# Linear attention and a SoLU block: chunks 5 to 8 computed on token rows, with a new order table

## The chip, the cores and the metric

The kernel runs on one core of a Trainium2 chip. Times are device microseconds of one execution. The engines named below are TensorE (PE; PEld is its weight load), VectorE (DVE), ScalarE (ACT), GpSimd (POOL) and SyncE (SP). POOL and SP also issue DMAs, and each runs its instructions in the order in which they stand.

## The reference

```python
def _attn_ref(q, k, v, g_norm):                    # (8, 8, 576, 64) each
    kv = np.einsum('bhsd,bhse->bhde', k, v)
    out = np.einsum('bhsd,bhde->bhse', q, kv)
    rms = np.sqrt(np.mean(out * out, axis=-1, keepdims=True) + 1e-06)
    return (out / rms * g_norm).astype(np.float32)

def _moe_ref(x, w_in, w_out, g_ln):                # x (4608, 512), d_ff 1024
    h = x @ w_in
    e = np.exp(h - np.max(h, axis=-1, keepdims=True))
    solu = h * e / (np.sum(e, axis=-1, keepdims=True) + 1e-09)
    mu = np.mean(solu, axis=-1, keepdims=True)
    var = np.mean((solu - mu) ** 2, axis=-1, keepdims=True)
    return ((solu - mu) / np.sqrt(var + 1e-06) * g_ln) @ w_out
```
The attention's output, transposed to tokens by heads, is x. All inputs and the output are FP32.

## The kernel before

The 4,608 tokens are nine chunks of 512. Chunk c below 8 holds, of batch c, eight of every nine tokens; chunk 8 holds the ninth of every batch. Loads (one k, v and q for each batch, batches 0 and 1 in halves a and b) are issued by POOL and cast to BF16 on the way; only the first k and v come by SP and ACT.

Every step is a named piece of a plan: its engine, a function, what it needs and which buffer slot it takes. A long string, ORDER, lists the pieces, and each engine's instructions stand in that order; a slot behind "@" and an engine behind "/" choose the buffer and the engine. So the table, written out, is the schedule. PSUM has three slots P of two banks and two slots S of one; SBUF has slots L, M, osq, lss, rst and ob.

The names, for chunk c (lines of the kernel before):
- kv (L310) is k^T v of a batch, kc its copy to `kvd`. qt and qc turn q by TensorE in chunks 0 to 4; qx (L366) turns it by a DMA on SP in chunks 5 to 8. ql copies a batch's last tokens to `q_last` for chunk 8.
- o (L403) is q kv with features on partitions, in two halves; sq (L416) squares it on ACT, s (L431) takes the head's mean by a matmul with `head_mean`, ln (L435) and ex (L439) make the reciprocal root on ACT, x (L449) multiplies on DVE and gives BF16, features on partitions, as the next matmul wants it.
- h is x w_in: by features in chunks 0 to 2 (L489), by rows in chunks 3 to 8 (L498), in four pairs of halves of four matmuls each. e is exp (L508, L515), u = h exp(h) (L523, L528), r its squares (L538 to L548), g the sums of e on POOL (L559, chunks 0 to 2), z the column sums (L607), st and rs the statistics.
- t (L553) turns u of chunks 3 to 8 by a DMA on SP. `gate` (L339), a one-element copy on POOL, needs q7, the last load; t3.0, and behind it every DMA transpose, waits for it, so that transposes start when the loads have landed.
- a (L678) is u times the centred w_out: four row blocks of two pieces of four matmuls; b scales it, d stores it (L703; SP, POOL or ACT).
- warm (L204) runs matmuls of zeros while the first loads are under way; wm (L661) takes the mean of w_out's columns, wc (L664) subtracts it on DVE.

In a transposed u of chunk c, column block m holds rows 2m and 2m+1 of nine in turn, so a store of 128 rows writes two neighbouring rows for each of 64 groups.

Of the kernel before, what the change touches and what calls it, by code (L numbers as in the profile page):

```python
# [24 lines left out]
QUADRANTS = ()  # L25

# [36 lines left out]
WARM = (13, 6, 2, 1)  # L63
# [27 lines left out]
ex4.01@rst1 x4.01 h3.01 h3.10@P2 h3.11 e3.0@M10 u3.0@L5 e3.1@M8 u3.1 a2.11 b2.1/act@ob6 kv5@P1 kc5.1/dve r3.0/dve
r3.1/dve o4.1@P0 sq4.10@osq1 d0.3/pool sq4.11@osq0 a2.20@S1 kc5.0/act a2.21 kc5.2/act s4.10@S0 ln4.10@lss0 s4.11@P2
ln4.11@lss1 ex4.10@rst1 ex4.11@rst0 h3.20@P1 h3.21 x4.10 x4.11 e3.2@M8 u3.2 h3.30@P2 h3.31 h4.00@P0 h4.01 h4.10@P1
e3.3@M11 u3.3 r3.2/act t3.0 qx5@M10 ql0/dve e4.0@M9 u4.0@L3 h4.11 e4.1@M0 a2.30@S0 d1.0/pool b2.2/act@ob3 o5.0@P2
sq5.00@osq0 a2.31 sq5.01@osq1 o5.1@P0 sq5.10@osq2 s5.00@S1 u4.1 b2.3/dve@ob2 h4.20@P1 qx6@M1 t3.1 t3.2 ln5.00@lss1
t3.3 t4.0@L4 r3.3/dve st3 sq5.11@osq0 d1.1/sp d1.2/sp d1.3/sp s5.01@S0 d2.0/pool ln5.01@lss0 ex5.00@rst0 x5.00@M11
ex5.01@rst1 s5.10@S1 ln5.10@lss1 x5.01 t4.1 h4.21 a3.00@S0 a3.01 e4.2@M10 u4.2 t4.2 ex5.10@rst1 s5.11@S1 ln5.11@lss0
qx7@M5 x5.10 h4.30@P2 ex5.11@rst0 h4.31 e4.3@M2 a3.10@S1 d2.1/sp x5.11 d2.2/pool kv6@P1 kc6.2/dve a3.11 r4.0/act
h5.00@P0 kc6.0/act kc6.1/dve o6.0@P1 u4.3 rs3 b3.0/dve@ob4 b3.1/act@ob3 sq6.00@osq0 sq6.01@osq2 r4.1/dve h5.01
e5.0@M9 h5.10@P2 s6.00@S0 s6.01@S1 ln6.00@lss0 ln6.01@lss1 ex6.00@rst0 ex6.01@rst1 u5.0@L2 x6.00@M0 x6.01 h5.11  # L100
# [15 lines left out]
d5.3/pool d6.0/sp d6.1/pool h8.10@P2 h8.11 a7.10@S1 e8.0@M7 e8.1@M5 u8.0@L3 r8.0/act b7.0/act@ob0 a7.11 h8.20@P1
d6.2/pool h8.21 e8.2@M7 u8.1 u8.2 h8.30@P0 h8.31 e8.3@M0 t7.3 t8.0@L2 t8.1 t8.2 u8.3 a7.20@S0 d6.3/pool d7.0/pool
r8.1/dve r8.2/dve a7.21 t8.3 r8.3/act st8 rs8 b7.1/act@ob0 a7.30@P2 a7.31 b7.2/dve@ob4 a8.00@P0 a8.01 a8.10@P1
b7.3/act@ob5 b8.0/dve@ob3 a8.11 b8.1/dve@ob2 a8.20@S0 a8.21 a8.3|0@S1 a8.3|1@P1 b8.2/act@ob1 d7.1/pool d7.2/sp
d7.3/pool d8.0/sp b8.3|0/act@ob4 b8.3|1/dve@ob3 d8.1/act d8.2/sp d8.3|0/sp d8.3|1/sp  # L120
# [4 lines left out]
def kernel(  # L125
# [16 lines left out]
    nc = tc.nc  # L142
# [43 lines left out]
    zeros = big.tile([128, 512], BF16, name="zeros")
# [43 lines left out]
    plan.add("gr", "sp", load_g)  # L230
    plan.add("ident", "pool", make_ident)
# [438 lines left out]
    for f in range(NF):  # L670
        plan.add(f"wc{f}", "dve", lambda f=f: w_center(f), ["wm"], uses=["mean", ("w_out", f // 4)])
# [88 lines left out]
```

## Time and profile before

| | us |
|---|---|
| median of 3 runs | 183.61 (183.49 to 184.53) |
| the profiled execution | 184.59 |
| its span, first to last instruction | 182.8 |
| mean granted TensorE clock | 0.971 |
| HBM read, written | 32.51 MB, 9.44 MB |

The profile gives the busy time of each engine, the chain of work that ended last, and the waits. What lies between 184.59 and 182.8 is outside of the span. Times in it are us from the span's start; "L498" is a line of the kernel. The busy time of matmuls is larger than the time that they take in a row, because they are pipelined: the chain counts them by their distance.

### The profile page before, as it was taken

The page shows a single profiled execution, that of the slowest core. Times are in us where ns is not written, and L with a number is a line of the kernel's source. Part 1 is how long each engine was busy: PE and PEld are TensorE (multiplying, and loading weights), DVE is VectorE, ACT ScalarE, POOL GpSimd, SP SyncE. Part 2 cuts the span into 40 slices and gives each one's busy share as a digit, 9 for nine tenths or more (in the row PEclk, how much of TensorE's full clock was granted, in tenths as well). Part 3 has the DMA queues.
Part 4 walks back from the last instruction along what each step waited for, and adds up shares of the span by engine and source line. Part 5 has one row for each costly group of instructions (what it writes and reads, how often), then busy time and mean ns, then how long its engine had stood idle before and what let it go on. Part 6 is the DMA issues. An engine that isn't in the chain of part 4 may idle for free.

```text
span 182.8 us, 4297 instructions
## 1 busy us (share of the span) xinstructions
PE 167.0 (91%) x1719; PEld 82.0 (45%) x1739; DVE 123.0 (67%) x230; ACT 136.0 (74%) x249; POOL 61.1 (33%) x77
## 2 busy tenths in 40 slices
PE   7697977899999999999949999999999999999991
PEld 2342446445455556445413444544444444444450
DVE  1327586866594778678855769757986989765841
ACT  2349765979897878979856999997994787957350
POOL 7851696723695997001310010300000111211020
PEclk9979996999999999999996999999999999999999
DMA  5999999999999999996899999893254999837655
GB/s 172 248 206 280 338 208 209 205 208 212 253 207 232 208 207 208 207 208 105 233 177 221 240 227 227 237 185 71 77 105 71 251 237 209 225 117 157 130 199 203
DMA packets 53591, 36.19 MB, mean 198 GB/s; under 512 B 35580, under 2 KB 48644, under 8 KB 53572
## 3 DMA queue, kind: packets, MB, share of 16 engines
q0 software_dynamic: 15696, 21.17, 58.1%
q1 hardware_dynamic: 37460, 13.90, 36.8%
q10 hardware_dynamic: 416, 0.85, 1.4%
q8 instruction: 13, 0.21, 0.4%
q14 instruction: 6, 0.05, 0.1%
HBM read 32.51 MB, written 9.44 MB: 229 GB/s over the span
## 4 chain that ended last, share of the span: by engine, by line
PE 80%; DMA 8%; DVE 4%; ACT 3%; issue 3%; ACTq 0%; POOLq 0%
PE ps_S L678 27%; PE ps_P L498 21%; PE ps_P L489 11%; PE ps_P L678 6%; DMA sb_M<-sb_M 4%; DMA sb_M<-in_q_dram 4%; PE ps_P L403 3%; PE ps_S L431 3%; PE ps_P L310 3%; DVE sb_M L449 2%; PE ps_S L355 2%; PE ps_P L204 2%; PE ps_S L607 1%; DVE w_out_sb L664 1%; PE ps_P L431 1%
## 5 line engine op out<-in xcount | busy, mean ns | idle before, releaser
L678 PE MATMUL ps_S<-w_out_sb,sb_L 128*128 128x512 bf16 x220 | 54.4, 379 | 1.1 <-issue 0.8
L498 PE MATMUL ps_P<-w_in_sb,sb_M 128*128 128x512 bf16 x190 | 45.2, 385 | 0.2
L678 PEld LDWEIGHTS <-sb_L 128*128 128x128 bf16 x280 | 26.4, 98 | 31.4 <-issue 1.2
L528 DVE SCALAR_TENSOR_TENSOR sb_L<-ps_P,sb_M 128x1024 bf16<-128x1024 f32 x24 | 29.3, 1223 | 11.4 <-ACT sb_M L515 10.9
L703 POOL DMA_DIRECT2D out_dram<-sb_ob x17 | 10.5, 617 | 78.9 <-ACT sb_ob L693 31.2
L449 DVE SCALAR_TENSOR_TENSOR sb_M<-ps_P,g_cols,sb_rst 128x512 bf16<-128x512 f32 x36 | 27.0, 788 | 8.6 <-ACT sb_rst L439 7.4
L515 ACT ACTIVATE sb_M<-ps_P 128x1024 f32<-128x1024 f32 x24 | 24.5, 1022 | 6.9 <-PE ps_P L498 6.7
L498 PEld LDWEIGHTS <-sb_M 128*128 128x128 bf16 x192 | 18.9, 99 | 23.2 <-issue 1.8
L416 ACT ACTIVATE sb_osq<-ps_P 128x512 bf16<-128x512 f32 x36 | 20.0, 595 | 4.7 <-PE ps_P L403 4.6
L489 PE MATMUL ps_P<-sb_M,w_in_sb 128*128 128x512 bf16 x93 | 22.0, 379 | 0.4 <-issue 0.2
L523 DVE TENSOR_TENSOR sb_L<-ps_P,sb_M 128x1024 bf16<-128x1024 f32 x12 | 14.7, 1224 | 8.8 <-ACT sb_M L508 8.6
L439 ACT ACTIVATE sb_rst<-sb_lss 128x512 f32<-128x512 f32 x32 | 19.3, 631 | 0.4
L559 POOL TENSOR_TENSOR sb_M<-sb_M 128x512 bf16<-128x512 f32 x12 | 15.3, 1276 | 4.1 <-issue 2.2
L508 ACT ACTIVATE sb_M<-ps_P 128x1024 f32<-128x1024 f32 x12 | 12.3, 1023 | 4.5 <-PE ps_P L489 4.5
L548 DVE SCALAR_TENSOR_TENSOR sb_M<-sb_L 128x1024 bf16<-128x1024 bf16 x13 | 15.5, 1218 | 0.0
L695 DVE TENSOR_SCALAR sb_ob<-ps_S,rstd 128x512 f32<-128x512 f32 x15 | 11.2, 748 | 6.3 <-PE ps_S L678 5.4
L435 ACT ACTIVATE sb_lss<-ps_S 128x512 f32<-128x512 f32 x23 | 13.4, 594 | 2.0 <-PE ps_S L431 1.9
L489 PEld LDWEIGHTS <-w_in_sb 128*128 128x128 bf16 x96 | 9.0, 97 | 11.5 <-issue 1.8
L693 ACT ACTIVATE sb_ob<-ps_S,rstd 128x512 f32<-128x512 f32 (+1 forms) x15 | 10.1, 671 | 3.7 <-issue 1.8
L546 ACT ACTIVATE sb_M<-sb_L 128x1024 bf16<-128x1024 bf16 x11 | 11.6, 1053 | 1.3 <-DVE sb_L L528 1.3
L431 PE MATMUL ps_S<-sb_osq,head_mean 128*128 128x512 bf16 x26 | 9.9, 407 | 1.3 <-ACT sb_osq L416 1.2
L678 PE MATMUL ps_P<-w_out_sb,sb_L 128*128 128x512 bf16 x47 | 11.0, 379 | 0.1
(85 smaller groups left out, 178.8 us busy)
## 6 DMA issues: line engine op xcount, KB each, us to landing
out_dram<-sb_ob SPq DMA_DIRECT2D x17, 256.0 KB, 3.9
out_dram<-sb_ob POOLq DMA_DIRECT2D x17, 256.0 KB, 4.1
sb_L<-in_k_dram POOLq DMA_DIRECT2D x6, 576.0 KB, 16.4
sb_L<-in_v_dram POOLq DMA_DIRECT2D x6, 576.0 KB, 18.5
sb_M<-in_q_dram POOLq DMA_DIRECT2D x6, 576.0 KB, 17.3
sb_L<-in_moe_w_out_dram POOLq DMA_DIRECT2D x2, 1024.0 KB, 15.5
sb_M<-in_q_dram POOLq DMA_DIRECT2D x4, 288.0 KB, 11.1
w_in_sb<-in_moe_w_in_dram POOLq DMA_DIRECT2D x2, 512.0 KB, 11.1
```

Source lines behind the costliest of these rows:

```text
L416: nc.scalar.activation(out=t[:, :], in_=T["o", c, hf][:, z], func=AF.Square)
L431: nc.tensor.matmul(t[:, 0], head_mean[:, :], T["osq", i][:, :], start=True, stop=True)
L439: nc.scalar.activation(out=t[:, :], in_=T["lss", i][:, :], func=AF.Exp, scale=-0.5)
L449: nc.vector.scalar_tensor_tensor(out=T["x", c][:, pairs_of(c, hf), :, z], in0=T["o", c, hf][:, z].rearrange("p (n q) -> p n q", n=2), scal ...
L489: nc.tensor.matmul(t[:, f % 2], w_in_sb[:, dt, f * 128:(f + 1) * 128], T["x", c][:, dt].rearrange("p q z -> p (q z)"), start=(dt == 0), st ...
L498: nc.tensor.matmul(T["h", c, m][:, half], T["x", c][:, dt].rearrange("p q z -> p (q z)")[:, m * 128:(m + 1) * 128], w_in_sb[:, dt, half * ...
L515: nc.scalar.activation(out=t.rearrange("p a b -> p (a b)"), in_=T["h", c, m].rearrange("p a b -> p (a b)"), func=AF.Exp, accum_out=T["zsum ...
L523: nc.vector.tensor_tensor(out=flat(T["u", c][:, 2 * p:2 * p + 2, :]), in0=flat(T["h", c, p]), in1=flat(T["e", c, p]), op=MUL)
L528: nc.vector.scalar_tensor_tensor(out=T["un", c][:, m, :], in0=T["h", c, m].rearrange("p a b -> p (a b)"), scalar=1.0, in1=T["e", c, m].rea ...
L548: nc.vector.scalar_tensor_tensor(out=unused, in0=src, scalar=1.0, in1=src, op0=MUL, op1=MUL, accum_out=by)
L559: nc.gpsimd.tensor_tensor(out=T["es", c][:, n, :], in0=e[:, 0, :], in1=e[:, 1, :], op=ADD)
L678: nc.tensor.matmul(T["acc", c, m][:, 0], T["u", c][:, f, m * 128:(m + 1) * 128], w_out_sb[:, f, :], start=(f == 0), stop=(f == NF - 1))
```

## The change

For chunks 5 to 8 (`ROWS_OF_X`) the attention's output is computed with tokens on partitions. The turned q is now the stationary operand and kv the moving one, 64 matmuls of 64 columns a chunk in two halves (`o_rows`). Each half is copied to SBUF (oc), squared (sq, POOL or ACT), summed over each head's 64 elements (vd, DVE), put through Ln and Exp on 16 numbers a row (vl, ACT), multiplied out with g_norm to a full tile (vg, POOL), multiplied on (x, two DVE products) to BF16 rows, and turned by a DMA on SP (xt), eight more transposes of 128 by 1024. The pieces s, ln and ex of these chunks go. g_norm is loaded once more, to all partitions (`gb`).

The turned x has its 512 columns in another order, so the stores of these chunks are two DMAs of 64 rows each. The zeros are FP32; warm0 multiplies them as FP32, the others read a BF16 view of half of it. w_out's mean is taken in two pieces, wm0 and wm1, each as its half has come, then copied to SBUF by ACT (mc), and wc reads that copy. ident is first on POOL. The table is new throughout: warm matmuls are (4, 4, 3, 3, 2, 2, 2, 5, 1) for (13, 6, 2, 1), kv4 to kv7 stand earlier, kv6 and kv7 ahead of `gate`, and o5.0 stands directly behind it.

```diff
+ROWS_OF_X = (5, 6, 7, 8)
-WARM = (13, 6, 2, 1)
+WARM = (4, 4, 3, 3, 2, 2, 2, 5, 1)
...
+        z = zeros[:, :] if i == 0 else zeros[:, 0:256].bitcast(BF16)
         for _ in range(WARM[i]):
-            nc.tensor.matmul(t[:, 0], zeros[:, 0:128], zeros[:, :], start=True, stop=True)
+            nc.tensor.matmul(t[:, 0], z[:, 0:128], z, start=True, stop=True)
...
+    def o_rows(c, hf):
+        t = T["o", c, hf] = bank(("o", c, hf))
+        o = t.rearrange("p x (m n r e) -> p x m n r e", m=2, n=2, r=2)
+        for mm in range(2):
+            for n2 in range(2):
+                for hh in range(2):
+                    for x in range(2):
+                        for jj in range(2):
+                            n, j = 2 * n2 + x, 2 * (2 * hf + mm) + jj
+                            at = (9 if c < B else 8) * n + j
+                            half = at % 2
+                            nc.tensor.matmul(
+                                o[64 * jj:64 * jj + 64, x, mm, n2, hh, :],
+                                T["qT", c][64 * half:64 * half + 64, at // 2, 64 * hh:64 * hh + 64],
+                                kv_of(c if c < B else j, n, hh ^ half)[64 * half:64 * half + 64],
+                                start=True, stop=True,
+                            )
...
+        t = T["oq", c, hf] = room(("oq", c, hf), [128, 1024], BF16)
...
+            nc.gpsimd.tensor_tensor(out=t[:, :], in0=src, in1=src, op=MUL)
...
+        nc.vector.tensor_reduce(
+            out=T["ms", c, hf][:, :], in_=T["oq", c, hf].rearrange("p (i e) -> p i e", e=D), op=ADD, axis=mybir.AxisListType.X
+        )
...
+        nc.gpsimd.tensor_tensor(
+            out=t[:, :, :], in0=T["rr", c, hf][:, :, None].to_broadcast([128, 16, D]),
+            in1=g_rep[:, None, :].to_broadcast([128, 16, D]), op=MUL,
+        )
...
+        for x in range(2):
+            nc.vector.tensor_tensor(
+                out=T["xr", c][:, 2 * hf:2 * hf + 2].rearrange("p m (n x) i -> p x m n i", x=2)[:, x],
+                in0=T["os", c, hf][:, x].rearrange("p (m n i) -> p m n i", m=2, n=2),
+                in1=T["rg", c, hf].rearrange("p (x m n r) e -> p x m n (r e)", x=2, m=2, n=2)[:, x], op=MUL,
+            )
...
+        nc.sync.dma_start_transpose(
+            T["x", c][:, two].rearrange("p m n i -> p (m n) i"), T["xr", c][:, two].rearrange("p m n i -> p (m n i)")
+        )
...
-            in1=T["mean"][:, 0], op0=MUL, op1=SUB,
+            in1=T["mean_sb"][:, :], op0=MUL, op1=SUB,
...
+            for jj in range(2):
+                queue.dma_start(rows_of(c, m)[jj][:, cols], T[key][64 * jj:64 * jj + 64, :])
```

More of the change, by code (lines that the diff above doesn't have):

```diff
@@ L91 @@
[L91 to L100, printed above, removed]
@@ L116 @@
[L116 to L120, printed above, removed]
+ident warm0@S0 k0a@L0,L1 v0a rsqrt q0a@M0 k0b v0b q0b wi0 wi1 cast0.0/act cast0.1/dve kv0a@P0 qt0.0@S0 wo0@L2
@@ new lines @@
+a2.00@S0 s4.10@S1 a2.01 kc6.0/dve rs2 b2.0/dve@ob1 kc6.1/act h3.20@P0 ln4.10@lss0 s4.11@S1 ex4.10@rst1 x4.10 h3.21
+h3.30@P1 r3.0/dve a2.10@S0 q7@M10 gb ln4.11@lss1 ex4.11@rst2 x4.11 e3.2@M7 h3.31 e3.3@M8 h4.00@P2 u3.2 d1.1/pool
+r3.1/dve h4.01 h4.10@P0 h4.11 u3.3 e4.0@M11 u4.0@L2 r3.2/act e4.1@M3 d1.2/pool d1.3/pool d2.0/pool ql3/pool a2.11
+ql6/pool b2.1/act@ob0 u4.1 a2.20@S1 a2.21 ql7/act b2.2/act@ob1 kv7@P2 kc7.2/dve kc7.0/dve gate@L6 t3.0 qx5@M1
+o5.0@P1 o5.1@P0 qx6@M7 r3.3/dve r4.0/act oc5.0/act@M1 st3 oc5.1/act@M11 a2.30@S1 r4.1/act a2.31 a3.00@S0
@@ new lines @@
+b2.3/act@ob4 sq5.0/pool@rst2 sq5.1/pool@rst1 kc7.1/dve o6.0@P1 o6.1@P0 oc6.0/dve@M12 sq6.0/pool@rst0 oc6.1/act@M3
+vd5.0 vd5.1 qx7@M9 h4.20@P2 h4.21 h4.30@P1 rs3 a3.01 vl5.0 e4.2@M10 u4.2 sq6.1/act@rst2 vd6.0 o7.0@P0 oc7.0/act@M7
+h4.31 e4.3@M6 vg5.0@M8 t3.1 t3.2 ql2/act t3.3 t4.0@L1 t4.1 a3.10@S1 a3.11 a3.20@P0 u4.3 a3.21 a3.30@P2 a3.31
+b3.0/act@ob5 d2.1/sp vl5.1 vg5.1@M2 vl6.0 r4.2/act b3.1/act@ob2 b3.2/act@ob3 b3.3/act@ob0 a4.00@S0 a4.01 o7.1@P0
+oc7.1/act@M9 qx8@M0 r4.3/dve sq7.0/pool@rst0 o8.0@P2 t4.2 vg6.0@M6 o8.1@P1 x5.0@M4 xt5.0@M1 a4.10@S1 vd6.1 st4 vl6.1
@@ L182 @@
     g_cols = big.tile([128, NF + 1], FP32, name="g_cols")
+    g_rep = big.tile([128, D], FP32, name="g_rep")
     ident = big.tile([128, 128], BF16, name="ident")
     eye = big.tile([NF + 1, NF + 1], FP32, name="eye")
[L186 removed]
+    zeros = big.tile([128, 512], FP32, name="zeros")
     nc.vector.memset(zeros, 0.0)
@@ new lines, in o_out, with o_rows_sq @@
+    def o_out(c, hf, engine):
+        t = T["os", c, hf] = room(("os", c, hf), [128, 2, 512], FP32)
+        copy(engine, t.rearrange("p x i -> p (x i)"), T["o", c, hf].rearrange("p x i -> p (x i)"))
+    def o_rows_sq(c, hf, engine):
+        t = T["oq", c, hf] = room(("oq", c, hf), [128, 1024], BF16)
+        src = T["os", c, hf].rearrange("p x i -> p (x i)")
+        if engine == "act":
+            nc.scalar.activation(out=t[:, :], in_=src, func=AF.Square)
+        else:
+            nc.gpsimd.tensor_tensor(out=t[:, :], in0=src, in1=src, op=MUL)
@@ new lines, in o_rows_sum, with o_rows_rms @@
+    def o_rows_sum(c, hf):
+        T["ms", c, hf] = small.tile([128, 16], FP32, name="ms")
+        nc.vector.tensor_reduce(
+            out=T["ms", c, hf][:, :], in_=T["oq", c, hf].rearrange("p (i e) -> p i e", e=D), op=ADD, axis=mybir.AxisListType.X
+        )
+    def o_rows_rms(c, hf):
+        lv = small.tile([128, 16], FP32, name="lv16")
+        nc.scalar.activation(out=lv[:, :], in_=T["ms", c, hf][:, :], func=AF.Ln, scale=1.0 / D, bias=1e-6)
+        T["rr", c, hf] = small.tile([128, 16], FP32, name="rr")
+        nc.scalar.activation(out=T["rr", c, hf][:, :], in_=lv[:, :], func=AF.Exp, scale=-0.5)
@@ L561 @@
     for c in range(NC):
-        xs = [[f"x{c}.{hf}{z}" for z in range(2)] for hf in range(2)]
+        xs = [[f"x{c}.{hf}{z}" for z in range(2)] for hf in range(2)] if c not in ROWS_OF_X else None
         if c in FEATURES_UP:
@@ L655, with w_mean, mean_copy @@
         plan.add(f"rs{c}", "act", lambda c=c: rstd(c), [f"st{c}"])
-    def w_mean():
-        t = T["mean"] = bank("mean")
-        for f in range(NF):
-            nc.tensor.matmul(t[:, 0], T["g_mean"][:, f, :], T["w_out", f // 4][:, f % 4, :], start=(f == 0), stop=(f == NF - 1))
+    def w_mean(half):
+        if half == 0:
+            T["mean"] = bank("mean")
+        for f in range(4 * half, 4 * half + 4):
+            nc.tensor.matmul(
+                T["mean"][:, 0], T["g_mean"][:, f, :], T["w_out", half][:, f % 4, :], start=(f == 0), stop=(f == NF - 1)
+            )
+    def mean_copy():
+        t = T["mean_sb"] = room("mean_sb", [128, d_model], FP32)
+        nc.scalar.copy(t[:, :], T["mean"][:, 0])
     def w_center(f):
```

134 lines of the change are left out of this document (88 added, 46 removed).

## The prediction

> **What bounds the kernel now.** I read the page's busy shares first, then the chain that ended last in order of time, then PE's waits, then one-microsecond windows around the only long wait.
>
> ```profile
> PE 167.0 (91%) x1719; PEld 82.0 (45%) x1739; DVE 123.0 (67%) x230; ACT 136.0 (74%) x249; POOL 61.1 (33%) x77
> ```
> TensorE is the busiest engine, so the question is what its remaining gaps wait for. The chain, in order of time (start us, us, what):
>
> ```profile
> 39.39 0.71 PE ps_P L310 x72
> ...
> 85.42 2.73 PE ps_P L498 x13
> 88.14 7.47 DMA sb_M<-sb_M
> 95.66 0.41 PE ps_P L403 x8
> ...
> 110.75 0.43 PE ps_S L431 x2
> 111.18 0.86 PE ps_P L498 x4
> ...
> 123.90 0.56 PE ps_P L403 x16
> ...
> 147.88 0.64 PE ps_P L403 x64
> ...
> 177.99 0.89 PE ps_P L685 x8
> 178.90 0.48 DVE sb_ob L695
> ```
> From 95.66 to 178.88 the chain is almost TensorE alone. A 512-column matmul costs 0.216 us there (4 in 0.86, head-mean matmuls L431 alike: 2 in 0.43). Before it stands one wait:
>
> ```profile
> PE ps_P L403 <- DMA sb_M<-sb_M: 2.5, 1, 2.5
> ```
> That is o5.0 waiting for qx5, the first q turned by DMA. What made qx5 late shows in the timeline of POOL and SP (start us, us, what) and in the windows behind it (us; PE, PEld, DVE, ACT, POOL busy; clock; DMA share; GB/s):
>
> ```profile
> 85.99 0.57 POOL L339 COPY sb_L<-sb_M 1x1 bf16<-1x1 bf16 x1 [12.97 <-ACT sb_lss L435]
> 86.51 1.84 POOL L703 DMA_DIRECT2D out_dram<-sb_ob  x3
> ```
>
> ```profile
> 86.59 1.37 SPq L553 DMA_TRANSPOSE sb_L<-sb_L  x1
> 88.14 8.32 SPq L366 DMA_TRANSPOSE sb_M<-sb_M  x2
> ```
>
> ```profile
> 84.00:85.00 1.00, 1.00 (x6) 0.45 (x5) 1.00 (x2) 0.99 (x3) 0.00 (x0) 1.00 0.68 115
> 85.00:86.00 1.00, 1.00 (x6) 0.48 (x5) 1.00 (x3) 0.78 (x3) 0.01 (x1) 1.00 0.11 18
> ```
> The load stream runs dry at about 84.8; the gate (L339, which waits for q7) starts at 85.99, frees t3.0 and then qx5, which lands 9.67 us after the gate (95.66 − 85.99). So the kernel has two halves: up to o5.0 the loads rule, from o5.0 on the sum of TensorE's work. A gain before o5.0 only lengthens the wait there, unless it moves work ahead of it or brings the gate forward.
>
> **The sum.** Counting the pieces of the two tables that stand at or behind o5.0: before, 49 four-matmul pieces of output, 36 of h, 16 head-mean matmuls, 8 o halves, kv6 and kv7. At 0.863, 0.863, 0.216, 0.34 and 0.71 us (last two: 16 matmuls of L403 in 0.56 to 0.68, 72 of L310 in 0.71) that is 42.3 + 31.1 + 3.5 + 2.6 + 1.4 = 80.9 us. The chain needed 178.88 − 95.66 = 83.2, so 2.3 us are lost, mostly to a clock that falls after the wait:
>
> ```profile
> 98.00:99.00 1.00, 1.00 (x3) 0.30 (x2) 1.00 (x4) 1.00 (x3) 0.00 (x0) 0.50 0.93 270
> 99.00:100.00 1.00, 1.00 (x4) 0.41 (x3) 0.40 (x4) 0.09 (x1) 0.00 (x0) 0.50 1.22 216
> ```
> After: 50 output pieces (one more), 36 of h, no head-mean matmul, kv6 and kv7 ahead of o5.0, and o as 64 matmuls of 64 columns a chunk. Chunk 8 ran in that form already, 64 in 0.64 us, so the new o of chunks 5 to 7 costs what the old did (0.68); in chunk 8 the row group now goes with the column group (both are jj), so two of the four quadrants are used, and the cost lies between 0.64 and 1.28; I take 1.0. Together 43.2 + 31.1 + 2.9 = 77.1: **3.8 us less behind o5.0** (16 head means 3.5, two kv 1.4, less one piece 0.9 and 0.2 for o).
>
> **When o5.0 starts.** DMA first. The order of loads is as before; ident goes ahead of q0a and delays three issues by under 1 us while k0a and v0a fill the engines, so nothing. But d0.3 and d1.0 now go out on SP while loads run, beside d0.0 to d0.2 in both kernels. A store is 262 KB; the best rate in a window with stores is 414 GB/s, 0.63 us each:
>
> ```profile
> 114.00:115.00 1.00, 1.00 (x37) 0.53 (x38) 0.96 (x2) 1.00 (x4) 0.00 (x0) 1.00 1.08 414
> ```
> Two delay q7 and the gate by 1.3, to 87.3. Behind the gate, before had three POOL stores (1.84 us of issue, 1.9 us of DMA) beside t3.0 and qx5; after, four stand ahead of the gate and drain behind q7. So qx5 lands 9.67 − 1.9 to 9.67 us after the gate; I take 8.7: o5.0 at 96.0 instead of 95.66. TensorE itself reaches it earlier: it had 73.2 us of work ahead and was done at 93.2; now 73.7, so near 93.8, with 2 us in hand for anything late in the first half. The FP32 zeros (4 matmuls of four passes for 13), the extra warm matmuls, the split mean, its copy by ACT and the new DVE order all lie there: kv2 ran at 39.39 just behind the landing of v2, which releases k5:
>
> ```profile
> 38.70 0.74 POOL L265 DMA_DIRECT2D sb_L<-in_k_dram  x1 [1.52 <-DMA sb_L<-in_v_dram]
> ```
> (in the built program each POOL DMA waits for the eighth before it: k5 for v2), so that half cannot get ahead of the loads either. I cost them at nothing; without the 2 us in hand each would count in full.
>
> **The row chain.** For c5 to c8, per half: oc (ACT or DVE, PSUM to SBUF), sq and vg on POOL, vd and x on DVE, vl on ACT, xt on SP. ACT loses 16 squares, Ln and Exp, and gains copies; it was not late behind o5.0, so this saves nothing by itself. What can be late is POOL, whose order is fixed, and SP. Their rows:
>
> ```profile
> L515 ACT ACTIVATE sb_M<-ps_P 128x1024 f32<-128x1024 f32 x24 | 24.5, 1022 | 6.9 <-PE ps_P L498 6.7
> ...
> L559 POOL TENSOR_TENSOR sb_M<-sb_M 128x512 bf16<-128x512 f32 x12 | 15.3, 1276 | 4.1 <-issue 2.2 <-ACT sb_M L508 1.8
> ...
> L540 POOL TENSOR_TENSOR sb_L<-sb_L 128x1024 bf16<-128x1024 bf16 x5 | 9.5, 1895 | 0.0
> ...
> L664 DVE SCALAR_TENSOR_TENSOR w_out_sb<-sb_L,g_cols,ps_S 128x512 bf16<-128x512 f32 x8 | 5.6, 742 | 0.1
> ```
>
> ```profile
> 104.72 2.91 SPq L553 DMA_TRANSPOSE sb_L<-sb_L  x2
> 107.73 2.94 SPq L366 DMA_TRANSPOSE sb_M<-sb_M  x1
> ```
>
> ```profile
> sb_L<-sb_L SPq DMA_TRANSPOSE x24, 3.3
> ```
> A 128x1024 FP32 product on POOL lies between 1.9 (L540) and 2.55 (twice L559); the form is L559's, I take 2.45. Counted from o5.0: oc5.0 is done at 1.7 (0.34 for o, 1.02 by L515, 0.3 to start), then ten POOL products up to vg6.1 and two stores (0.6 each) end at 1.7 + 24.5 + 1.2 = 27.4; vd and vl run while POOL is at another half's product; x6.1 (two DVE products, 0.7 each by L664) 28.8; xt6.1 lands 3.3 later, 32.1. TensorE wants h6.20 after 32.3 us of work, about 34 with the slow clock: 1.9 us to spare. SP: 0.8 to finish qx6, qx7 2.94, five t at 1.45, a store, qx8 at up to 2.94, t4.2, then xt5.0 issued at 15.9 and landed at 19.2; h5.00 is wanted at 18.4 + 1.7 = 20.1. Both fit, barely; I charge 0.5 for what doesn't.
>
> No row shows POOL contended: behind the gate it only issued stores. The Trainium skill, GPSIMD Engine Reference, section Key points, says that GpSimd shares its SBUF interfaces with VectorE and contends with VectorE instructions that have two SBUF inputs. That speaks against this change, since x and w_center are now such instructions; if the six x products (4.2 us) that fall in the ten POOL products stopped POOL outright, the sum would be 4.2 − 1.9 − 0.5 = 1.8 us worse, an estimate by that page. No row of before shows it.
>
> **Tail.** Each store of chunks 5 to 8 is two DMAs. Only the last counts: after the 0.48 scale, one more issue on SP, 0.6 (1.84 for three above). The earlier ones hide beside matmuls.
>
> Sum: TensorE ends at 96.0 + 77.1 + 2.3 + 0.5 = 175.9, 3.0 us earlier than 178.9; with 0.6 of tail 2.4 us less. The profiled execution took 184.59 (span 182.8), so 182.2 for it; it lay 1.0 above the median of 183.61, so the forecast is **181.2**. The bounds (qx5 0.9 either way, chunk 8's o 0.3, stalls 0 to 2, the slow clock 0.8 to 2.3) give it 179.3 to 183.2.
>
> **Rivals.** *POOL becomes the bound* (slower). Its place is sq5.0 to vg6.1, in order, with xt7.0, xt7.1 and then t5.1 behind xt6.1 on SP. It decides from 2.64 us a product; every 0.1 more is 1 us. For: the products are twice the width of L559's and no row has one beside VectorE work on two SBUF tensors; against: L559 and L540 kept 1.28 and 1.9 with VectorE at its exp products. At 3.3 a product TensorE stalls 10 × 0.85 − 1.9 = 6.6, so 181.2 − 0.5 + 6.6 = 187.3.
>
> *The gate goes late.* In after POOL has g2.0, g2.1, r2.2, r2.3, g2.2, g2.3 and a small copy between v7 and q7: 4 × 1.28 + 2 × 1.9 = 8.9 us and a little. v7 waits for q5, eight DMAs earlier; with v3 landed at 47.2 and a load each 2.85 us (590 KB at 207 GB/s), q5 lands at 67.1:
>
> ```profile
> 47.20 0.74 POOL L265 DMA_DIRECT2D sb_L<-in_k_dram  x1 [2.30 <-DMA sb_L<-in_v_dram]
> ```
>
> ```profile
> 68.00:69.00 1.00, 1.00 (x10) 0.53 (x8) 0.64 (x1) 1.00 (x2) 1.00 (x1) 1.00 1.21 207
> ```
> So q7 issues near 77 and v7 lands near 81.4: 4 us of cover. POOL 9 us later would cost 5: 186.2.
>
> *The gate's shadow shrinks* (faster): o5.0 at TensorE's own arrival, 94.3, and no slow clock: 1.7 + 1.5 less, 178.0. For it: the stores leave the transposes alone. Against: the windows from 98 to 100, transposes only, moved 270 and 216 GB/s. The Trainium skill, Advanced Engine Details and Errata, section X-Bar Transpose (TRN2), expects 350 to 400 GB/s of a transpose, by which a q of 590 KB would take an estimated 1.5 to 1.7 us; those two windows disagree.
>
> *The head means' time is taken back* by small waits of the new order: 183.3.
>
> **Chances.** Forecast 0.42, POOL 0.22, late gate 0.12, shorter shadow 0.16, taken back 0.08. The range reaches to the two outer cases, 178.0 to 187.3, and leaves out the half of each that lies beyond, 0.19. A change under 1% (1.8 us) can't be told from none here. Faster by over 1% is 181.77 or less: three quarters of the forecast and the shorter shadow, 0.48; slower (185.45 or more) is POOL and two thirds of the late gate, 0.30; the rest, 0.22, lies within.
>
> **What would show it.** Right: 16 fewer head-mean matmuls, and none behind o5.0; one DMA wait of TensorE at o5.0 ending near 96; 80 us from there to the last matmul; POOL products near 2.45. Wrong: a TensorE wait for xt (h6.20 above all) longer than 1 us; DMA share under 0.5 before the gate; the gate later than 88.5; o5.0 reached by TensorE after qx5 has landed.

## The result: 11.6% slower

The changed kernel took 205.43 us (median of 4 runs, 204.59 to 206.63), the kernel before beside it 184.07 us (183.49 to 184.72): a ratio of 1.1164, 95% interval 1.1086 to 1.1242. The profiled execution took 204.92 us, its span is 203.1 us, the granted clock 0.966. The forecast was 181.2. Ratios here and below are of fast executions alone, while the medians also count those over 1.5% above their kernel's fastest, so a median can lie above what its ratio gives.

The page's busy shares come first:

```profile
PE 173.2 (85%) x1875; PEld 82.8 (41%) x1875; DVE 146.2 (72%) x221; ACT 126.5 (62%) x237; POOL 108.8 (54%) x111
```
VectorE is busy 23 us longer than before (146.2 against 123.0) with nine instructions fewer. GpSimd is busy 48 us longer, with the work that the change gives it. Next the groups by line, engine and shape (busy us, mean ns of one, then the idle time before them):

```profile
L512 DVE TENSOR_TENSOR sb_M<-sb_M,sb_M 128x512 bf16<-128x512 f32 x16 | 22.2, 1430 | 0.8 <-DMA sb_M<-sb_M 0.8
...
L763 DVE SCALAR_TENSOR_TENSOR w_out_sb<-sb_L,g_cols,sb_rst 128x512 bf16<-128x512 f32 x8 | 13.5, 1730 | 0.4 <-ACT sb_rst L760 0.4
...
L726 DVE TENSOR_TENSOR f<-a,qsum 128x4 f32<-128x4 f32 x6 | 4.2, 702 | 0.1
```

```profile
L503 POOL TENSOR_TENSOR sb_M<-rr,g_rep 128x1024 f32<-128x1024 f32 x8 | 17.0, 2124 | 21.0 <-ACT rr L499 19.0 <-ACT sb_M L638 1.3 <-DVE sb_M L512 0.7
...
L487 POOL TENSOR_TENSOR sb_rst<-sb_M 128x1024 bf16<-128x1024 f32 x7 | 13.7, 1957 | 13.2 <-ACT sb_M L173 11.4 <-DVE sb_M L175 1.8
```
L763 is w_center: 742 ns before, 1730 now, for the same 512 elements. L512 is the new x, twice the 0.7 us of the prediction. L726 multiplies four numbers a partition and takes 702 ns. GpSimd's products, L503 and L487, are faster than the 2.45 us that the prediction took. So the engine whose instructions became longer is VectorE. The timeline of VectorE and GpSimd (start us, us) shows one case:

```profile
28.30 3.87 DVE L763 SCALAR_TENSOR_TENSOR w_out_sb<-sb_L,g_cols,sb_rst 128x512 bf16<-128x512 f32 x1
```

```profile
28.47 1.93 POOL L632 TENSOR_TENSOR sb_L<-sb_L 128x1024 bf16<-128x1024 bf16 x1
30.33 1.28 POOL L651 TENSOR_TENSOR sb_M<-sb_M 128x512 bf16<-128x512 f32 x1
```
One w_center lasts from 28.30 to 32.17, across two products of GpSimd, and ends 0.6 us after the second (31.61). The stretches of 5 us, first of the kernel before, then of the changed one (us; PE, PEld, DVE, ACT, POOL busy; clock; DMA share; GB/s), show what this does to TensorE:

```profile
30.00:35.00 5.00, 3.84 (x96) 2.78 (x86) 2.82 (x9) 4.18 (x10) 3.63 (x5) 0.76 1.21 207
120.00:125.00 5.00, 4.95 (x37) 2.23 (x36) 3.27 (x6) 4.33 (x10) 0.00 (x0) 1.00 0.93 186
```

```profile
30.00:35.00 5.00, 1.20 (x39) 0.67 (x39) 5.00 (x4) 1.00 (x2) 3.29 (x3) 1.00 1.21 208
120.00:125.00 5.00, 3.24 (x100) 1.89 (x85) 4.97 (x5) 1.44 (x3) 5.00 (x3) 1.00 0.55 129
```
In both places VectorE counts as busy all the time, with four or five instructions in 5 us, and TensorE waits. TensorE's waits (us in total, times, longest us) name VectorE, or the turn of x behind it:

```profile
PE ps_P L589 <- DMA sb_M<-sb_M: 5.0, 3, 2.2
PE ps_P L589 <- DVE sb_L L620: 4.8, 2, 3.7
PE ps_P L359 <- DVE sb_L L615: 4.3, 1, 4.3
```
The place that was the border of the two halves, o5.0 behind the gate, in TensorE's timeline:

```profile
101.42 0.84 PE L470 MATMUL ps_P<-kvd,sb_M 64*64 64x64 bf16 x64
```
o5.0 starts at 101.42, 5.8 us later than before, and without a wait (the row would end in its releaser): TensorE itself is late. From there to the end of the span are 101.7 us, before 87.1 (182.8 − 95.66). So 5.8 us are lost ahead of o5.0 and 14.5 behind it, 20.3 in all.

### The profile page after: what moved, and what is told of

Read it like the earlier page. It is cut to its first block, busy times and chain, and to the rows that moved or that the text cites. A ratio compares the mean times of both kernels' runs of the same rounds, so it can differ in the third digit from the quotient of the medians.

```text
span 203.1 us, 4653 instructions
## 1 busy us (share of the span) xinstructions
PE 173.2 (85%) x1875; PEld 82.8 (41%) x1875; DVE 146.2 (72%) x221; ACT 126.5 (62%) x237; POOL 108.8 (54%) x111
## 5 line engine op out<-in xcount | busy, mean ns | idle before, releaser
L589 PE MATMUL ps_P<-w_in_sb,sb_M 128*128 128x512 bf16 x192 | 47.0, 393 | 11.9 <-DMA sb_M<-sb_M 5.0
L620 DVE SCALAR_TENSOR_TENSOR sb_L<-ps_P,sb_M 128x1024 bf16<-128x1024 f32 x24 | 29.0, 1219 | 8.3 <-ACT sb_M L607 8.1
L607 ACT ACTIVATE sb_M<-ps_P 128x1024 f32<-128x1024 f32 x24 | 24.4, 1017 | 12.1 <-DVE sb_M L512 6.5
L503 POOL TENSOR_TENSOR sb_M<-rr,g_rep 128x1024 f32<-128x1024 f32 x8 | 17.0, 2124 | 21.0 <-ACT rr L499 19.0
L512 DVE TENSOR_TENSOR sb_M<-sb_M,sb_M 128x512 bf16<-128x512 f32 x16 | 22.2, 1430 | 0.8 <-DMA sb_M<-sb_M 0.8
L632 POOL TENSOR_TENSOR sb_L<-sb_L 128x1024 bf16<-128x1024 bf16 x10 | 18.9, 1898 | 3.9 <-DVE sb_L L615 3.9
L487 POOL TENSOR_TENSOR sb_rst<-sb_M 128x1024 bf16<-128x1024 f32 x7 | 13.7, 1957 | 13.2 <-ACT sb_M L173 11.4
L453 DVE SCALAR_TENSOR_TENSOR sb_M<-ps_P,g_cols,sb_rst 128x512 bf16<-128x512 f32 x20 | 15.3, 791 | 7.0 <-ACT sb_rst L443 5.1
L615 DVE TENSOR_TENSOR sb_L<-ps_P,sb_M 128x1024 bf16<-128x1024 f32 x12 | 14.5, 1221 | 7.6 <-ACT sb_M L600 7.5
L638 ACT ACTIVATE sb_M<-sb_L 128x1024 bf16<-128x1024 bf16 x17 | 17.8, 1050 | 3.3 <-DVE sb_L L620 3.3
L812 POOL DMA_DIRECT2D out_dram<-sb_ob x14 | 7.3, 531 | 21.7 <-ACT sb_ob L795 20.4
L795 ACT ACTIVATE sb_ob<-ps_S,rstd 128x512 f32<-128x512 f32 x16 | 10.9, 683 | 9.1 <-PE ps_S L780 6.2
L797 DVE TENSOR_SCALAR sb_ob<-ps_S,rstd 128x512 f32<-128x512 f32 (+1 forms) x13 | 9.5, 727 | 9.0 <-DMA out_dram<-sb_ob 5.0
L600 ACT ACTIVATE sb_M<-ps_P 128x1024 f32<-128x1024 f32 x12 | 12.1, 1028 | 4.4 <-PE ps_P L580 3.5
L763 DVE SCALAR_TENSOR_TENSOR w_out_sb<-sb_L,g_cols,sb_rst 128x512 bf16<-128x512 f32 x8 | 13.5, 1730 | 0.4 <-ACT sb_rst L760 0.4
L580 PEld LDWEIGHTS <-w_in_sb 128*128 128x128 bf16 x96 | 9.0, 98 | 11.6 <-issue 2.0
```

The source lines that it names most:

```text
L453: nc.vector.scalar_tensor_tensor(out=T["x", c][:, pairs_of(c, hf), :, z], in0=T["o", c, hf][:, z].rearrange("p (n q) -> p n q", n=2), scal ...
L503: nc.gpsimd.tensor_tensor(out=t[:, :, :], in0=T["rr", c, hf][:, :, None].to_broadcast([128, 16, D]), in1=g_rep[:, None, :].to_broadcast([1 ...
L512: nc.vector.tensor_tensor(out=T["xr", c][:, 2 * hf:2 * hf + 2].rearrange("p m (n x) i -> p x m n i", x=2)[:, x], in0=T["os", c, hf][:, x]. ...
L580: nc.tensor.matmul(t[:, f % 2], w_in_sb[:, dt, f * 128:(f + 1) * 128], T["x", c][:, dt].rearrange("p q z -> p (q z)"), start=(dt == 0), st ...
L589: nc.tensor.matmul(T["h", c, m][:, half], T["x", c][:, m, dt] if c in ROWS_OF_X else T["x", c][:, dt].rearrange("p q z -> p (q z)")[:, m * ...
L607: nc.scalar.activation(out=t.rearrange("p a b -> p (a b)"), in_=T["h", c, m].rearrange("p a b -> p (a b)"), func=AF.Exp, accum_out=T["zsum ...
```

## The experiments

Theory A: a VectorE instruction that reads two tensors in SBUF stands still while GpSimd multiplies. That holds up w_center in the first half and x and the statistics in the second. Rival B: the new order, the longer row chain, SyncE's queue and the split stores cost the time. Rival C: GpSimd is late by its own added work.

**The mean read in PSUM again.** In the changed kernel (two warm-up pieces then take another bank, and wc7 stands ahead of s1.00):

```diff
-            in1=T["mean_sb"][:, :], op0=MUL, op1=SUB,
+            in1=T["mean"][:, 0], op0=MUL, op1=SUB,
...
-    plan.add("mc", "act", mean_copy, ["wm1"], [("rst", "mean_sb")], ["mean"])
```

> The changed kernel with one operand put back: w_center reads the mean in PSUM again, the copy to SBUF is left out (two warm-up pieces take another bank, wc7 goes ahead of s1.00). Theory A (VectorE with two SBUF tensor operands stands still while GpSimd multiplies): the eight w_center fall from a mean of 1730 ns to about 740, PE's idle stretch at 30 to 40 us shrinks by some 9 us, the q load behind it and the gate come some 7 us earlier (gate at 86 to 88 instead of 93.8), and the time is 196 to 199 us. Rival B (the order and the longer row chain cost the time): about 205 us, w_center still above 1.2 us. Rival C (GpSimd is late by its own added work r and g): w_center falls, the gate stays after 92 us, about 204 us.

201.18 us, ratio 1.0888 (1.0792 to 1.0984). The group of w_center, and o5.0 in TensorE's timeline:

```profile
L712 DVE SCALAR_TENSOR_TENSOR w_out_sb<-sb_L,g_cols,ps_S 128x512 bf16<-128x512 f32 x8 | 5.5, 741 | 0.0
```

```profile
96.67 0.85 PE L419 MATMUL ps_P<-kvd,sb_M 64*64 64x64 bf16 x64
```
w_center is back at 741 ns and o5.0 starts 4.75 us earlier; from o5.0 to the end are 102.1 us, as in the changed kernel. So this edit brings back 4.75 of the 5.8 us ahead of o5.0 and nothing behind it. The gain was expected at 6 to 9 us; it is 4.3, and the gate comes at 88.8, not 86 to 88.

**That operand alone in the kernel before.**

```diff
+    plan.add("mc", "act", mean_copy, ["wm"], [("rst", "mean_sb")], ["mean"])
-            in1=T["mean"][:, 0], op0=MUL, op1=SUB,
+            in1=T["mean_sb"][:, :], op0=MUL, op1=SUB,
```

> The kernel before with that one operand alone: ScalarE copies the mean to SBUF and w_center reads the copy; nothing else is changed. Theory A: w_center goes from 742 ns to 1.2 to 1.8 us wherever GpSimd multiplies beside it, 4 to 8 us more in that stretch, and the time goes from 184 to 187 to 192 us. Rival B: no change, 184 us, or 0.7 us more for the copy.

185.42 us, 1.0059 (1.0024 to 1.0095). Its group and, from GpSimd's timeline, what ran beside it:

```profile
L668 DVE SCALAR_TENSOR_TENSOR w_out_sb<-sb_L,g_cols,sb_rst 128x512 bf16<-128x512 f32 x8 | 5.7, 757 | 1.1 <-ACT sb_rst L665 1.1
```

```profile
25.66 1.26 POOL L559 TENSOR_TENSOR sb_M<-sb_M 128x512 bf16<-128x512 f32 x1
26.87 0.81 POOL L265 DMA_DIRECT2D sb_L<-in_k_dram  x1
```
This missed the 187 to 192 us that theory A gave, and sharpens the theory: w_center starts at 26.6, when GpSimd's last product is ending (26.9) and its loads begin. An operand in SBUF costs next to nothing by itself (757 ns against 742), and the loads that GpSimd issues do not hold w_center here. If theory A is right, a product must run beside it. The next two kernels bring one there, with the mean in SBUF and in PSUM:

```diff
-r0.0/act@L4 r0.1/act
+r0.0/pool@L4 r0.1/pool
...
-r0.3/act
+r0.3/pool
```

> The kernel before with the mean copied to SBUF, and with three squares of chunk 0 (r0.0, r0.1, r0.3) on GpSimd instead of ScalarE, so that GpSimd multiplies beside w_center. Theory A: the w_center beside a product take 1.2 to 2 us and more, a mean of 1.1 to 1.5 us against 757 ns without the products, and the time is 2 to 6 us above its twin with the mean in PSUM. Rival B: w_center at 740 to 760 ns, both twins alike.

> The twin: the kernel before with r0.0, r0.1 and r0.3 on GpSimd, the mean read in PSUM as before. Theory A: w_center at 742 ns although GpSimd multiplies beside it; the loads queued behind the 5.7 us of products come later by at most 4 us, 184 to 188 us. Rival B: as the one with the copy.

191.52 us (1.0364, 1.0321 to 1.0407) with the copy, 188.45 (1.0203, 1.0169 to 1.0236) without it. The two groups:

```profile
L668 DVE SCALAR_TENSOR_TENSOR w_out_sb<-sb_L,g_cols,sb_rst 128x512 bf16<-128x512 f32 x8 | 11.0, 1409 | 0.2 <-ACT sb_rst L665 0.2
```

```profile
L664 DVE SCALAR_TENSOR_TENSOR w_out_sb<-sb_L,g_cols,ps_S 128x512 bf16<-128x512 f32 x8 | 5.6, 741 | 0.1
```
The same GpSimd products, the same order; 1409 ns with the operand in SBUF, 741 in PSUM, and 3.1 us of the whole, of which the copy by itself accounts for about 1.1 (the 0.6% of the run before). GpSimd pays too, by its timeline, first in the kernel with the copy, then in its twin:

```profile
27.89 2.34 POOL L540 TENSOR_TENSOR sb_L<-sb_L 128x1024 bf16<-128x1024 bf16 x1
30.19 1.71 POOL L559 TENSOR_TENSOR sb_M<-sb_M 128x512 bf16<-128x512 f32 x1
```

```profile
26.78 1.89 POOL L540 TENSOR_TENSOR sb_L<-sb_L 128x1024 bf16<-128x1024 bf16 x1
28.63 1.26 POOL L559 TENSOR_TENSOR sb_M<-sb_M 128x512 bf16<-128x512 f32 x1
```
Each of its products is 0.45 us longer. The two engines take turns.

**No product on GpSimd behind the gate**, and then both edits together. In the changed kernel, for chunks 5 to 8:

```diff
-sq5.0/pool@rst2 sq5.1/pool@rst1
+sq5.0/act@rst2 sq5.1/act@rst1
...
-        nc.gpsimd.tensor_tensor(
+        nc.vector.tensor_tensor(
             out=t[:, :, :], in0=T["rr", c, hf][:, :, None].to_broadcast([128, 16, D]),
```

> The changed kernel with GpSimd's two products behind the gate given away: all squares sq go to ScalarE, all eight vg to VectorE (1024 FP32 elements, some 1.1 us each); the first half is left as it is. Theory A: the x products fall from a mean of 1430 ns to about 690, the 128x4 statistics from 700 to about 160, PE's stalls behind o5.0 fall from 14 to 16 us to about 4 to 6, and although VectorE has 9 us and ScalarE 8 us more to do the time is 192 to 196 us. Rival B (the chain's length and the order): x stays late since VectorE and ScalarE have more to do, 205 us or more.

> Both of the preceding edits in the changed kernel: the mean read in PSUM, and no product on GpSimd behind the gate. Theory A: the two losses add, so the gains do: 9 us in front of the gate and 10 behind it, 182 to 187 us, about the time before. Rival B: above 200 us. Rival C: the gate stays after 92 us, 192 to 196 us.

197.54 us (1.0659, 1.058 to 1.0739) alone, 192.0 us (four executions from 189.94 to 195.36; 1.0284, 1.018 to 1.0388) with the mean in PSUM. Both times lie above what theory A gave (192 to 196 and 182 to 187). From the groups of the first:

```profile
L512 DVE TENSOR_TENSOR sb_M<-sb_M,sb_M 128x512 bf16<-128x512 f32 x16 | 10.3, 684 | 0.0
L503 DVE TENSOR_TENSOR sb_M<-rr,g_rep 128x1024 f32<-128x1024 f32 x8 | 9.7, 1219 | 0.1
...
L726 DVE TENSOR_TENSOR f<-a,qsum 128x4 f32<-128x4 f32 x6 | 1.0, 162 | 0.1
```
x falls from 1430 to 684 ns and the four-number product from 702 to 162, as theory A said. VectorE takes over eight products of 1.22 us and is still busy for less time: x alone gives back 11.9 us (22.2 − 10.3). Laid out by the border at o5.0, from the spans and the starts of o5.0 in the profiled executions (us):

| | o5.0 starts | from there to the end | span |
|---|---|---|---|
| before | 95.66 | 87.1 | 182.8 |
| changed | 101.42 | 101.7 | 203.1 |
| mean in PSUM | 96.67 | 102.1 | 198.8 |
| no product behind the gate | 102.16 | 92.2 | 194.4 |
| both | 96.22 | 92.0 | 188.2 |

Each edit acts on its own half and leaves the other as it was to within 0.8 us; together they bring back 14.9 of the 20.3 us. The edit behind the gate does two things at once: it ends the contention, and it gives the row chain's two products to quicker engines (the second takes 1219 ns on VectorE, 2124 on GpSimd), which shortens that chain. TensorE's waits behind o5.0 that name VectorE fall from 8.7 us with the mean in PSUM to 3.8 with both edits, those for the turned x from 4.9 to 0.4; how much of the latter is contention and how much the shorter chain was not tried apart. The combined kernel is still slower than before; those 5.4 us (188.2 − 182.8, the profiled execution being the fastest of its four) are what rival B can still claim.

**The cost by itself.** A kernel that runs one VectorE form beside six GpSimd products, stretch by stretch (eight instructions of each form, six of the reduction):

> Not the kernel but the disputed cost by itself: it computes nothing of the reference and stores zeros. Twelve stretches, begun together on VectorE and GpSimd: VectorE runs one form (two FP32 operands in SBUF; one of them in PSUM; one SBUF operand, FP32 and BF16; two BF16 operands in SBUF; a reduction; 128x4 with two operands in SBUF) alone or beside six GpSimd products of 128x1024 FP32, beside six GpSimd copies, and beside four loads that GpSimd issues. Theory A: alone 0.68 to 0.74 us for 512 elements; beside products the forms with two SBUF operands stand still until a product ends (maxima of 1.9 us or more, the eight of them as long as the products, 128x4 too), the forms with an operand in PSUM or with one SBUF operand keep their time, and the product stays at 1.89 to 1.96 us in every stretch; beside loads nothing changes. The traces do not tell what a GpSimd copy with one operand does. Rival D (the two engines share bandwidth and both slow down): every SBUF form is some 1.5 to 2 times as long beside products, 128x4 no longer than 0.2 us, and the product itself rises above 2.2 us.

VectorE's timeline, one row per stretch; the first is two SBUF operands alone, the next five stand beside products, the last two beside six GpSimd copies and beside loads:

```profile
7.64 5.76 DVE L65 TENSOR_TENSOR do<-fa,fb 128x512 bf16<-128x512 f32 x8
...
34.65 17.87 DVE L65 TENSOR_TENSOR do<-fa,fb 128x512 bf16<-128x512 f32 x8
...
52.56 6.23 DVE L68 SCALAR_TENSOR_TENSOR do<-fa,col,pm 128x512 bf16<-128x512 f32 x8
...
67.46 15.75 DVE L71 CAST do<-fa 128x512 bf16<-128x512 f32 x8
...
119.48 7.48 DVE L80 TENSOR_REDUCE ms<-ba 128x16 f32<-128x1024 bf16 x6
...
134.42 7.61 DVE L83 TENSOR_TENSOR do<-fa,fb 128x4 bf16<-128x4 f32 x8
```

```profile
149.36 10.06 DVE L65 TENSOR_TENSOR do<-fa,fb 128x512 bf16<-128x512 f32 x8
...
159.45 5.77 DVE L65 TENSOR_TENSOR do<-fa,fb 128x512 bf16<-128x512 f32 x8
```
GpSimd's timeline, for its products alone and beside the form with two SBUF operands:

```profile
20.13 14.41 POOL L56 TENSOR_TENSOR po<-ga,gb 128x1024 f32<-128x1024 f32 x6
...
35.45 16.53 POOL L56 TENSOR_TENSOR po<-ga,gb 128x1024 f32<-128x1024 f32 x6
```
The single durations of the 128x4 product (min/median/max in ns):

```profile
L83 DVE TENSOR_TENSOR do<-fa,fb x8: 151/162/2191, 134.4 to 139.8; 128x4 bf16<-128x4 f32 x8
```
Two SBUF operands: 5.76 us alone, 17.87 beside products, 5.77 beside loads. An operand in PSUM (L68, 6.23 us alone too) and the reduction (L80, 1.22 us each, 1.21 in the changed kernel without products behind the gate) don't notice the products. Of the eight 128x4 products most slip through in 0.16 us, but the longest took 2.19. Against theory A as it stood, a plain copy with one SBUF operand (L71) is held as well: 15.75 us for eight, of which the quickest took 0.417 us. The two BF16 forms are held too: 15.76 us for eight copies, 15.72 for six products of two operands. GpSimd's six products lose only 2.1 us beside the first form (16.53 for 14.41) and 4.5 at most (18.92, beside the BF16 products). Alone each takes 2.34 us, not the 1.89 to 1.96 that was expected. Rival D, shared bandwidth, falls: 128x4 would hardly feel that, yet one of them took 2.19 us, and L68 kept its time. The Trainium skill, SBUF — State Buffer, section SBUF: two separate sides, describes an exclusive lock on a shared pair of ports: GpSimd, or a VectorE instruction with two SBUF inputs or in a two-port mode, whichever starts first, has it for the whole instruction. Turns of whole instructions, copies included, are what these rows show.

**What is left.** The next kernels start from the one with both edits. First g_norm goes into w_in (in place, 1.28 us of VectorE between the matmuls of chunks 4 and 5) and vg goes; then r2.2 and r2.3 go to ScalarE as well:

```diff
+        nc.vector.tensor_scalar_mul(
+            out=w_in_sb.rearrange("p n f -> p (n f)"), in0=w_in_sb.rearrange("p n f -> p (n f)"), scalar1=g_cols[:, NF:NF + 1]
+        )
...
-r2.2/pool r2.3/pool
+r2.2/act r2.3/act
```

> The kernel with both edits (mean in PSUM, no GpSimd product behind the gate), and the product rr times g taken away altogether: g of the head norm is multiplied once into w_in in place, on VectorE between the last matmul of chunk 4 and the first of chunk 5, and x is o times rr. That leaves out eight products of 1.22 us on VectorE. Theory A goes on: what is left behind the gate in the kernel with both edits is VectorE full (9.8 to 9.9 of 10 us at 110 to 120 and 130 to 140) with PE waiting for u and x there, so PE's stalls behind o5.0 (about 9 us in all) fall by 3 to 5 and the time goes from 192 to 186 to 188 us. Rival E (what is left is the chain's length and SyncE's queue of turns): 190 us or more, the stalls only move.

> The same with two squares of chunk 2, r2.2 and r2.3, on ScalarE instead of GpSimd, where they stand ahead of the last q load: that load was issued at 77.6 us in the kernel with both edits against 72.3 us before, and the gate came at 88.4 instead of 86.0. Rival C (GpSimd is late by its own added squares) now stands for the rest of the lateness: the q load at 73 to 75, the gate at 85 to 87, 1.5 to 2.5 us less than without this edit, 184 to 186 us. If ScalarE (8.3 of 10 us busy at 60 to 80) becomes late by it, no gain.

190.41 us (1.033, 1.0246 to 1.0413) and 190.67 us (1.0402, 1.0309 to 1.0495): no gain over 1.0284 that these runs can tell, and neither reaches what was hoped for (186 to 188, 184 to 186). Stretches of 10 us, with both edits and then with g folded in:

```profile
130.00:140.00 10.00, 7.78 (x36) 3.32 (x35) 9.94 (x19) 7.90 (x17) 0.31 (x1) 1.00 0.42 105
...
150.00:160.00 10.00, 10.00 (x48) 4.58 (x47) 7.09 (x14) 5.42 (x12) 3.16 (x6) 1.00 1.11 186
```

```profile
130.00:140.00 10.00, 9.04 (x42) 3.97 (x41) 9.10 (x20) 8.56 (x18) 0.62 (x1) 1.00 0.47 117
...
150.00:160.00 10.00, 8.68 (x40) 3.84 (x40) 4.43 (x10) 4.54 (x11) 2.79 (x6) 1.00 1.11 185
```
TensorE's 1.3 us at 130 to 140 come back as a loss of 1.3 at 150 to 160: the stalls move, as rival E said. In the other kernel q7 was issued at 74.1 instead of 77.6, and the gate still started at 88.8: on GpSimd a store that waits for b2.0 and two copies stand ahead of it. TensorE did not wait at o5.0 either way, so the late gate, which is rival C, does not set the time.

Then SyncE's queue: qx8 behind qx7 instead of behind five turns of u, and five stores moved to GpSimd; after that the store d2.1 directly behind the gate, and d2.2 and d2.3 on GpSimd; after that the first three squares on GpSimd again.

```diff
-ql7/act
+ql7/act ql2/act
-qx7@M9
+qx7@M9 qx8@M0
...
-gate@L6
+gate@L6 d2.1/pool
...
-sq5.0/act@rst2 sq5.1/act@rst1
+sq5.0/pool@rst2 sq5.1/pool@rst1
```

> The kernel with the mean in PSUM, g folded into w_in and r2.2, r2.3 on ScalarE, now with SyncE's queue changed: the turn of chunk 8's q (qx8) stands right behind qx7 instead of behind five turns of u and a store (its last copy, ql2, goes earlier on ScalarE), and the stores d5.3 and d6.0 to d6.3 go to GpSimd's queue. Rival E (what is left of the loss is SyncE's queue): PE's wait of 2.0 us at o8.0 and its 0.6 us on the last turns of u go, 188.0 us or less against 190.7. If the turn of q only pushes the turns of u back, PE waits as long at a3.1 or a4.0 instead, and the time stays within 1 us of 190.7.

> The preceding kernel with the store d2.1 on GpSimd right behind the gate instead of on SyncE behind the turns of q and u, and d2.2, d2.3 on GpSimd. In the preceding kernel ScalarE's b3.3 stood 3.1 us until the store from the same output buffer had landed, and o8.0 waited 2.4 us for the bank that b3.3 reads. If this chain is what is left at o8.0, the wait goes and the time falls by 1.5 to 2.5 us, to 187.5 to 188.6. If ScalarE is late anyway (9.9 of 10 us busy at 100 to 110), o8.0 still waits over 1 us and the time stays above 189.

> The same with the first three squares (sq5.0, sq5.1, sq6.0) back on GpSimd, at a place where VectorE runs copies and products that read PSUM and reductions, and one pair of statistics. Theory A: nothing is held but the few small operations, x keeps about 690 ns, ScalarE has 3 us less to do at 100 to 110, and the time is the same or up to 1.5 us lower, 186.5 to 188.5 us. Rival D (any product on GpSimd slows VectorE): x and the reductions above 1.3 us there, and the time rises by 1 us or more.

190.11 us (1.0305, 1.0218 to 1.0393), 191.82 us (1.039, 1.0318 to 1.0461), 193.71 us (1.0505, 1.0432 to 1.0579): none brings the gain that was hoped for. In the first, TensorE's wait at o8.0 only changed its cause. The row of the kernel without the edit, then with it:

```profile
116.41 1.20 PE L419 MATMUL ps_P<-kvd,sb_M 64*64 64x64 bf16 x64 [1.97 <-DMA sb_M<-q_last]
```

```profile
117.11 1.20 PE L419 MATMUL ps_P<-kvd,sb_M 64*64 64x64 bf16 x64 [2.40 <-ACT sb_ob L742]
```
In the second that wait is gone, but the turns of q on SyncE, now with stores beside them, took longer, here without and with the early stores:

```profile
90.61 10.01 SPq L319 DMA_TRANSPOSE sb_M<-sb_M  x3
100.72 1.94 SPq L319 DMA_TRANSPOSE sb_M<-q_last  x1
```

```profile
90.42 11.55 SPq L319 DMA_TRANSPOSE sb_M<-sb_M  x3
102.08 4.63 SPq L319 DMA_TRANSPOSE sb_M<-q_last  x1
```
In the third the squares stood beside copies out of PSUM, reductions and one set of statistics. That set was held (VectorE's and TensorE's timelines):

```profile
99.28 1.82 DVE L674 TENSOR_TENSOR f<-a,qsum 128x4 f32<-128x4 f32 x1
101.13 1.82 DVE L676 SCALAR_TENSOR_TENSOR vare<-f,d 128x4 f32<-128x4 f32 x1
```

```profile
103.46 2.75 PE L537 MATMUL ps_P<-w_in_sb,sb_M 128*128 128x512 bf16 x11 [1.22 <-DVE kvd L124]
```
Two instructions of 0.16 us held VectorE for 3.6 us; the kv copy queued behind them made TensorE wait 1.2 us. x stayed at 685 ns and the reductions at 1213, so rival D fails here too. The expectation called the small operations nothing; they explain 1.2 of the 1.9 us more (193.71 − 191.82), and the rest was not traced.

Intervals of neighbours among the three overlap; only the third lies clear of the first. No version beats the kernel before.

## Why the prediction was wrong

- **The step that failed: "two DVE products, 0.7 each by L664", and with it "I cost them at nothing" for w_center's new operand.** L664 had one operand in PSUM; both new instructions have two in SBUF, and GpSimd multiplies beside them. Measured: 1430 and 1730 ns. Undoing the two places brings back 4.75 us ahead of o5.0 and 9.5 behind it (101.7 − 92.2), of which the shorter row chain may hold a part. The prediction named the contention but let it stop only GpSimd, by 1.8 us, and only at six x products. VectorE stops far longer than GpSimd (12.1 us more for eight of its products, 2.1 for GpSimd's six), and all that stands behind in its queue with it: u, which TensorE's matmuls wait for, and x, which the turns wait for. Three of the prediction's own signs of being wrong showed: TensorE waited up to 2.2 us for a turned x, the gate came after 88.5, and TensorE reached o5.0 after qx5 had landed.
- **GpSimd's product at 2.45 us** was too high: 2.12 and 1.96. The rival "POOL becomes the bound", from 2.64 a product, did not happen, though its sign was right.
The last points need TensorE's busy time on both sides of o5.0 (us; PE busy; clock; DMA share; GB/s), in the kernel before and then in the one with both places undone:

```profile
0.00:95.66 95.66, 84.62 (x1108) 0.96 1.13 216
95.66:182.80 87.14, 82.41 (x611) 0.98 0.79 178
```

```profile
0.00:96.22 96.22, 88.37 (x1267) 1.00 1.13 225
96.22:188.20 91.98, 79.50 (x632) 0.99 0.95 182
```
- **o5.0 at 96.0.** With both places undone it is at 96.22, so the time held but for the contention; the reason did not. There was no wait at o5.0 and so no "2 us in hand": TensorE's busy time ahead of o5.0 is 88.4 us there, 84.6 before, 3.8 more where the prediction had 0.5 (73.7 for 73.2). How they divide between the FP32 zeros, the warm matmuls and the moved kv was not tried.
- **"3.8 us less behind o5.0".** TensorE's busy time from o5.0 to the end is 79.5 us with both places undone, 82.4 before: 2.9 less. The head means' matmuls did go, and the direction was right. But before, the granted clock was 0.50 from 98 to 100, and with both places undone it is 1.00 there; so about 1 us of the 2.9 is the clock (an estimate: half of 2 us), and the 3.8 are not confirmed. By its own prices the sum gives 3.7: the new o is 3 × 0.68 + 1.0 = 3.0, not 2.9, and the old one 2.7, not 2.6, by six halves at 0.34 and chunk 8 at 0.64, which leaves 0.4 for o, not 0.2.
- **"I charge 0.5 for what doesn't" fit** was mis-sized even without the lock: with both places undone TensorE idles 12.5 us from o5.0 to the end (92.0 − 79.5), before 4.7 (87.1 − 82.4). Without the tails behind the last matmul, 4.4 and 3.9, that is 8.1 against 0.8. This is where the forecast gain went and most of the remaining 5.4 us. Five kernels tried to remove it, and none became faster. It has no single cause that the runs name; that stays open.
- **The gate's lateness** came true (93.79 for 87.3) and was not what counted, as TensorE arrived later still.
- **Tail, 0.6 more:** in the changed kernel 4.5 us from the end of the last matmul to the end of the span, before 3.9. The size was right; that the added store is the cause was not tried.

## What to carry to other kernels

Before work is given to GpSimd, list what VectorE runs in the same stretch: in these runs instructions with two operands in SBUF, and plain copies between SBUF tensors, stood until the GpSimd product beside them had ended, even one of 0.16 us, and everything behind them in VectorE's queue waited too. Keep one operand in PSUM where it already is; a copy to SBUF that frees the bank early can cost more than it gains. A duration is only a price for an instruction whose operands lie where those of the measured one lay.

## What the runs showed of the hardware

- A GpSimd product of a BF16 tensor with itself, 128x1024, took 1.89 us where VectorE did not hold it; of two different FP32 tensors 2.34 us (14.41 us for six in a row).
- GpSimd copies of 128x1024 also hold VectorE: eight products of two SBUF operands took 10.06 us beside six copies, 5.76 alone.
- A VectorE multiplication by a column of 4096 BF16 elements in place took 1.28 us, hardly longer than one that writes 1024 FP32 elements from two operands in SBUF (1.22).
